# Where the W1 weights of a fused attention and MLP block are split: four pieces in the prologue, nineteen in the value stage, five in the Q and K stage

## The chip, the core and the metric

The kernel runs on one core of one Trainium2 chip. The metric is the time of one execution on the device, in microseconds (us). The core has TensorE (PE; PEld is its weight load), VectorE (DVE), ScalarE (ACT), GpSimd (POOL) and SyncE (SP), which mostly issues DMAs. Transfers are issued on the queues of SP and ACT and run on 16 DMA engines.

## The reference

For a sequence of 2048 tokens of width 1024, with 32 heads of 32 and an MLP of width 3584:

```python
xn = _layernorm(x, axis=-1)
s = _A_ref(xn, A_wqkv, A_wo)          # softmax attention, 32 heads, then @ wo
g = _silu(_B_ref(xn, B_w1, B_b1, B_w2))   # h = xn @ w1 + b1; mish(h) @ w2
return x + s * g
```

All inputs are float32.

## The kernel before

Every float32 matrix product is done as three products of a reduced float32 format (F32R): each operand is split into a high part (a copy that rounds) and a low part (the operand minus the high part, `low`), and high x high, high x low and low x high are added. Weights are split once, stored in DRAM in split form, and read back when needed. The first linear layer's weight W1 has 28 pieces (`FT`) of 1024 x 128: a piece is 512 KB raw and 1 MB split, in `w1s[f]`. W2 is split into 14 groups (`u`), of seven tiles each (`pw2`), because the second layer uses a scheme with seven products of half blocks.

The kernel has these stages.

- **Prologue** (to about 72 us). For each of 16 tiles of 128 tokens `t`: x is loaded on SP (`x_load`, a ring of five buffers), DVE takes mean and variance (`ln_a`: two bn_stats, one bn_aggr, one add), ACT the reciprocal root (`ln_r`), DVE corrects it by four instructions on one column (`ln_b`, lines 369 to 372), ACT normalizes (`ln_x`), PE transposes (`ln_t`), and ACT and DVE write the split xn into the chunk tile `xc[t // 4]` (`ln_c`: two copies, two subtracts). `xc[c]` holds 512 tokens, high part in `[:, 0]`, low part in `[:, 1]`. In between PE computes the first quarter of V (`v_group(0, ..)`). From t = 8 on, finished chunks are stored to DRAM (`xs`).
- **Value stage** (to 214 us). The other three quarters of V, `for i in range(1, 4)`, 16 groups each of 24 matmuls. After each group, `w1_early(step)` does a part of splitting W1 piece f = step // 2: on even steps it loads piece f and splits piece f - 1 on POOL (two casts and two subtracts, `split_w(.., job=True)`); on odd steps it stores the split piece. The split form goes into a buffer from `w_tile`, which hands out two places in turn: `z0` in the pool `w1p` and `w` in the pool `big`. The split Q and K weights (`qkw`) take their buffers from the same two. `W1_V = 21` pieces are done here.
- **Q and K stage** (to 640 us). 16 weight tiles f by 4 chunks c: `qk_group(f, c)` is 24 matmuls; ACT copies the result to `qst` (two buffers), DVE makes the low part, and ACT issues the store. After group (f, 0) ACT and DVE split the next weight tile (`qk_split(f + 1)`) and ACT issues the load of the one after it. Beside this POOL splits W2 group u = f (`w2_parts`, steps 0 to 3 after groups 0 to 3) for f up to 13, and half a W1 piece after each of the first 2 x (28 - 21) = 14 weight tiles (`presplit`: a load of 256 KB, a cast, a subtract, a store of 512 KB). For f of 12 and more PE also does four score matmuls of head 0 after each group.
- **The long stage** (from 640 us). Attention scores, exponentials, the MLP and the output product run together in an order that a planner in the program works out beforehand from fixed costs. The last part multiplies with Wo and forms the output.

The order of the work in the first three stages is the order in which the program is written. Each engine takes its instructions in that order. The DMAs of SP and ACT together, in program order, take eight completion semaphores in turn, and a DMA waits until the one before it on the same semaphore has landed; so a DMA of ACT can wait for one that SP issued eight places earlier, and the other way round. `later.at(n, fn)` moves an issue n groups on.

Of the kernel before, what the change touches and what calls it, by code (L numbers as in the profile page):

```python
# [9 lines left out]
F32 = mybir.dt.float32  # L10
F32R = mybir.dt.float32r
# [7 lines left out]
P = 128  # L19
KT = D // P  # L20
# [3 lines left out]
SCALE = DH ** -0.5  # L24
EPS = 1e-5

W1_V = 21
NS = H * NT
U = FT // 2

# [191 lines left out]
def body(ctx: ExitStack, tc: tile.TileContext, x, wqk, wv, wo, w1, b1, w2, out):  # L222
    nc = tc.nc
# [6 lines left out]
    def pool(stack, name, bufs, side="left", **kw):  # L230
        return stack.enter_context(tc.tile_pool(name=name, bufs=bufs, side=side, reuse_waits="tile", **kw))
# [8 lines left out]
    w1s = [dram.tile([P, 2, 2, KT // 2, P], F32R, name=f"w1s{i}") for i in range(FT)]  # L240
# [26 lines left out]
    w1p = pool(low_, "w1p", 1)  # L267
# [5 lines left out]
    def copy(out_, in_, scale=1.0):  # L273
        nc.scalar.activation(out_, in_, AF.Copy, scale=scale)  # L274

    def move(out_, in_, eng=None):

        (eng or nc.sync).dma_start(out_.bitcast(F32), in_.bitcast(F32))

    def low(eng, out_, in_, high):  # L280

        eng.tensor_tensor(out_, in_, high.bitcast(F32), ALU.subtract)  # L282
# [5 lines left out]
    def w_tile(name):  # L288
        w_made.append(name)
        where, tag = ((w1p, "z0"), (big, "w"))[len(w_made) % 2]  # L290
        return where.tile([P, 2, 2, KT // 2, P], F32R, tag=tag, name=name)
# [5 lines left out]
    big = pool(ph, "big", 1)  # L297
    ps1 = psum(ph, "ps1", 8)
    xc = [xc0] + [big.tile([P, 2, KT, 512], F32R, name=f"xc{c}") for c in range(1, NC)]
# [5 lines left out]
    def v_load(i):  # L305
        raws = []
        for half in range(2):
            raw = vp.tile([P, 4, 256], F32, tag="x", name=f"vraw{i}_{half}", bufs=5)
            nc.sync.dma_start(raw, wv[i][:, half * 4:half * 4 + 4])
            raws.append(raw)  # L310
        return raws
# [27 lines left out]
    def x_load(t):  # L339
        xt = vp.tile([P, D], F32, tag="x", name=f"x{t}", bufs=5)  # L340
        nc.sync.dma_start(xt, x[t * P:(t + 1) * P, :])
        return xt

    xts = {t: x_load(t) for t in range(2)}
    vraw = v_load(0)
    xts[2] = x_load(2)
# [19 lines left out]
    def ln_b(t):  # L366
        mv, var, rs = stat.pop(t)
        tmps[t] = tmp = vp.tile([P, 1], F32, tag="tmp", name=f"tmp{t}", bufs=3)
        nc.vector.scalar_tensor_tensor(tmp, rs, var, rs, op0=ALU.mult, op1=ALU.mult)
        nc.vector.tensor_scalar(tmp, tmp, -0.5, 1.5, op0=ALU.mult, op1=ALU.add)  # L370
        nc.vector.tensor_tensor(rs, rs, tmp, ALU.mult)
        nc.vector.scalar_tensor_tensor(tmp, mv[:, 0:1], -1.0, rs, op0=ALU.mult, op1=ALU.mult)
        tmps[t] = tmp, rs
# [44 lines left out]
    for t in range(2, NT + 2):  # L418
        if t < NT:
            ln_b(t)  # L420
        evac = v_group(0, vw, t - 2, 12 if t == 2 else 8, (lambda: ln_t(t - 1)) if t <= NT else None)
        if t <= NT:
            ln_c(t - 1)
        if t < NT:
            ln_x(t)
        for m in (4, 5, 6) if t == 2 else (t + 4,):
            if m < NT:
                xts[m] = x_load(m)
        if t == 2:
            ln_a(3)  # L430
        if t + 2 < NT:
            ln_a(t + 2)
        if t + 1 < NT:
            ln_r(t + 1)
        evac()
        if t == NT - 3:
            vraw = v_load(1)
        if t > 7:
            c, k = t // 4 - 1, t % 4 * 2
            move(xs[c][:, :, k:k + 2], xc[c][:, :, k:k + 2])  # L440
        if t == NT:
            nvw = v_split(1, vraw)
            vraw = v_load(2)
# [6 lines left out]
        raws[f] = big.tile([P, KT, P], F32, tag="raw", name=f"qkraw{f}")  # L450
        (nc.scalar if f > 1 else nc.sync).dma_start(raws[f], wqk[f])

    def split_w(w, raw, job=False):
        for half in range(2):
            r = slice(half * 4, half * 4 + 4)
            if job:
                nc.gpsimd.tensor_copy(w[:, half, 0], raw[:, r])
            else:
                copy(w[:, half, 0], raw[:, r])
            low(nc.gpsimd if job else nc.vector, w[:, half, 1], raw[:, r], w[:, half, 0])  # L460

    qkw = {}

    def qk_split(f):
# [4 lines left out]
    early_w1 = {}  # L469

    def w1_early(step):
        f, late = divmod(step, 2)
        if not late:
            if f < W1_V:
                raw = vp.tile([P, KT, P], F32, tag="x", name=f"w1e{f}", bufs=5)
                nc.sync.dma_start(raw, w1[f])
                early_w1[f] = [raw, None]
            if 0 < f <= W1_V:
                raw, _ = early_w1[f - 1]
                early_w1[f - 1][1] = w = w_tile(f"w1p{f - 1}")  # L480
                split_w(w, raw, True)
        elif 0 < f <= W1_V:
            move(w1s[f - 1], early_w1.pop(f - 1)[1])

    for i in range(1, 4):
        vw = nvw
# [107 lines left out]
    sp = pool(qb, "sp", 2, side="right")  # L594
    jobs = iter([(f, half) for f in range(W1_V, FT) for half in range(2)])

# [71 lines left out]
    for f in range(2 * KT):  # L668
        for c in range(NC):
            qk_group(f, c if f < 2 * KT - 1 else (c + 1) % NC)  # L670
            if f < U:
                w2_parts(f, c)
                if c == 3 and f + 2 < U:
                    later.at(1, lambda u=f + 2: w2_load(u))
            if c == 3 and f < 2 * (FT - W1_V):
                presplit()
# [690 lines left out]
    for c in range(NC):  # L1367
        for s in range(4):
            t = 4 * c + s
            if t + 4 < NT:  # L1370
                start(t + 4)
            for dh in range(2):
                k = 2 * s + dh
# [4 lines left out]
                if c:  # L1378
                    n = 2 * s + dh
# [53 lines left out]
```

## Time and profile before

| | |
|---|---|
| median of 3 runs | 3469.04 us (3467.42 to 3472.01) |
| profiled execution | 3470.76 us, span from first to last instruction 3469.0 us |
| PE busy | 3376.7 us, 97% of the span |
| POOL busy | 2792.7 us, 81% |
| DVE busy | 2614.4 us, 75% |
| ACT busy | 2017.0 us, 58% |
| DMA traffic | 639.92 MB, mean 184 GB/s |

Busy shares are means over stages with different limits, so the profile is read by stages here. A row of a group reads: line, engine, operation, what it writes and reads, shapes, count, then busy us and mean ns of one, then the idle time before it and what ended it. A row of the timeline begins with its start and its duration in us; the bracket at its end is the idle time of the engine before it and what released it. `SPq` and `ACTq` are the queues on which DMAs are issued.

### The profile page before, as it was taken

What the parts mean: (1) busy time and instruction counts of PE and PEld (TensorE: products, weight loads), DVE (VectorE), ACT (ScalarE), POOL (GpSimd) and SP (SyncE); (2) the same over time, 40 slices, a digit from 0 to 9 for tenths busy, and PEclk for the clock granted to TensorE, in tenths of its full rate; (3) what the DMA queues carried; (4) which work ended last, traced back from release to release, by engine and by line L of the source; (5) the groups of instructions that cost most, each with busy time, mean ns of one, the idle gap of its engine ahead of it and who ended that gap; (6) DMA issues with size and microseconds to landing.
All of it is one profiled execution on the core that took longest, in us unless ns stands there. A gap on an engine that the chain in (4) does not pass through costs nothing.

```text
span 3469.0 us, 48684 instructions
## 1 busy us (share of the span) xinstructions
PE 3376.7 (97%) x17491; PEld 2474.8 (71%) x17491; DVE 2614.4 (75%) x4382; ACT 2017.0 (58%) x3360; POOL 2792.7 (81%) x1033
## 2 busy tenths in 40 slices
PE   8999898999999999999999999999999999999999
PEld 8987676776776666666677666666766666667687
DVE  6012124799999998888989988888999889996653
ACT  6111111476766666767667667666766777677621
POOL 0749984489898888998989899989988999999910
PEclk9999998999999999999999999999999999999999
DMA  8869997444555556554545664445546545556582
GB/s 293 318 240 346 348 359 251 137 138 131 147 152 153 153 149 210 156 154 139 153 138 158 195 183 140 134 134 152 153 146 189 178 138 152 150 160 192 165 308 85
DMA packets 255189, 639.92 MB, mean 184 GB/s; under 512 B 89994, under 2 KB 99210, under 8 KB 244106
## 3 DMA queue, kind: packets, MB, share of 16 engines
q1 hardware_dynamic: 233076, 587.52, 54.6%
q10 hardware_dynamic: 21872, 49.29, 3.9%
q8 instruction: 139, 2.28, 0.3%
q14 instruction: 102, 0.84, 0.1%
HBM read 474.97 MB, written 160.69 MB: 183 GB/s over the span
## 4 chain that ended last, share of the span: by engine, by line
PE 78%; POOL 8%; DVE 6%; DMA 4%; ACT 2%; issue 1%; SPq 1%; ACTq 0%; POOLq 0%; DVEq 0%
PE h L982 16%; PE y L1123 13%; PE pv L871 12%; PE s L736 12%; PE t L823 12%; PE v L329 5%; PE op L1250 4%; POOL pw L282 3%; PE qk L657 3%; DVE mx L742 2%; POOL pw L625 1%; POOL tmp L636 1%; DMA kstack<-ks 1%; POOL z L852 1%; DVE yacc L1146 1%
## 5 line engine op out<-in xcount | busy, mean ns | idle before, releaser
L852 POOL TENSOR_TENSOR z<-z,p 128x2048 f32<-128x2048 f32 x448 | 2067.1, 4614 | 74.7 <-ACT p L271 50.2
L271 ACT ACTIVATE p<-t,zero 128x512 f32<-128x512 f32 x2048 | 1366.1, 689 | 457.2 <-PE t L823 436.9
L742 DVE TENSOR_REDUCE mx<-s 128x1 f32<-128x512 f32 x1984 | 1284.1, 683 | 67.7 <-PE s L736 65.3
L823 PE MATMUL t<-qstack,kstack 128*128 128x512 f32 x2048 | 791.7, 394 | 1.8 <-ACT p L271 0.9
L736 PE MATMUL s<-kstack,qstack 128*128 128x512 f32 x1984 | 756.1, 397 | 16.2 <-DMA kstack<-ks 7.3
L982 PE MATMUL h<-xr,w 128*128 128x512 f32 x2016 | 677.3, 390 | 1.5 <-DVE aw L282 0.6
L1146 DVE TENSOR_TENSOR yacc<-yacc,y 128x512 f32<-128x512 f32 x728 | 493.0, 680 | 40.4 <-PE y L1123 36.9
L736 PEld LDWEIGHTS s<-kstack,qstack 128*128 128x128 f32 x1984 | 367.0, 188 | 163.0 <-issue 31.5
L823 PEld LDWEIGHTS t<-qstack,kstack 128*128 128x128 f32 x2048 | 381.8, 188 | 126.4 <-issue 28.5
L871 PE MATMUL pv<-p,v 128*32 128x512 f32 x4096 | 467.2, 596 | 1.3 <-ACT p L271 0.6
L982 PEld LDWEIGHTS h<-xr,w 128*128 128x128 f32 x2016 | 377.9, 188 | 84.7 <-DVE aw L282 2.1
L657 PE MATMUL qk<-xc,qkw 128*128 128x512 f32 x1536 | 368.9, 401 | 29.6 <-ACT qkw L274 26.3
L657 PEld LDWEIGHTS qk<-xc,qkw 128*128 128x128 f32 x1536 | 296.6, 194 | 99.1 <-ACT qkw L274 29.3
L852 POOL TENSOR_TENSOR z<-p,p 128x2048 f32<-128x2048 f32 x32 | 147.8, 4620 | 217.5 <-PE zp L907 111.9
L871 PEld LDWEIGHTS pv<-p,v 128*32 128x32 f32 x4096 | 120.1, 110 | 277.7 <-issue 248.6
L282 DVE TENSOR_TENSOR qst<-qk,qst 128x512 fp32r<-128x512 f32 x64 | 44.3, 692 | 307.6 <-ACT qst L274 307.6
L274 ACT ACTIVATE qst<-qk 128x512 fp32r<-128x512 f32 x64 | 38.3, 598 | 370.5 <-PE qk L657 97.5
L1123 PE MATMUL y<-w,az 128*128 128x512 f32 x672 | 232.5, 395 | 4.2 <-POOL az L282 1.6
L1123 PE MATMUL y<-w,ay 128*128 128x512 f32 x672 | 229.0, 395 | 3.5 <-ACT ay L274 1.4
L1123 PE MATMUL y<-w,ax 128*128 128x512 f32 x672 | 224.8, 391 | 2.6 <-DVE yacc L1146 1.4
L982 PE MATMUL h<-xc,w 128*128 128x512 f32 x672 | 225.9, 391 | 0.0
L329 PE MATMUL v<-vw,xc 128*128 128x256 f32 x1536 | 190.8, 285 | 2.7 <-POOL vw L282 1.5
(117 smaller groups left out, 3659.9 us busy)
## 6 DMA issues: line engine op xcount, KB each, us to landing
w<-w2s SPq DMA_DIRECT2D x392, 512.0 KB
w<-w1s SPq DMA_DIRECT2D x224, 512.0 KB
w2s<-pw SPq DMA_DIRECT2D x98, 512.0 KB
qstack<-qs SPq DMA_DIRECT2D x96, 256.0 KB
kstack<-ks SPq DMA_DIRECT2D x96, 256.0 KB
w1s<-w1p SPq DMA_DIRECT2D x21, 1024.0 KB
x<-in_A_x_dram SPq DMA_DIRECT2D x32, 512.0 KB
qs<-qst ACTq DMA_DIRECT2D x32, 512.0 KB
```

What stands on the lines that cost most here:

```text
L271: nc.scalar.activation(out_, in_, fn, bias=zero if bias is None else bias, scale=scale)
L282: eng.tensor_tensor(out_, in_, high.bitcast(F32), ALU.subtract)
L329: nc.tensor.matmul(ps[:, :256], xc[t // 4][:, a, k, (t % 4) * P:(t % 4 + 1) * P], w[:, b, k], start=n == 0, stop=n == 3 * KT - 1)
L657: nc.tensor.matmul(ps, w[:, k // 4, a, k % 4], xc[c][:, b, k], start=n == 0, stop=n == 3 * KT - 1)
L736: nc.tensor.matmul(sp_, qst[h % 3][:, qt * P:(qt + 1) * P], kst[h % 3][:, kc * 512:(kc + 1) * 512], start=True, stop=True)
L742: nc.vector.reduce_max(tiles["mx"][:, qt, kc:kc + 1], tiles[qt, kc], axis=AX.X)
L823: nc.tensor.matmul(tp, kst[h % 3][:, kt * P:(kt + 1) * P], qst[h % 3][:, c * 512:(c + 1) * 512], start=True, stop=True)
L852: nc.gpsimd.tensor_tensor(zs[h], pts[T - 1] if kt == 1 else zs[h], pts[T], ALU.add)
L871: nc.tensor.matmul(t["b"][c * DH:(c + 1) * DH, :], vt[h][:, k, :], pts[T - kt + k][:, c * 512:(c + 1) * 512], start=k == kt - size + 1, st ...
L982: nc.tensor.matmul(t["h"], w1t[m_][:, a, k % 4], xts_[c][:, b, k], start=i == 0, stop=i == 3 * KT - 1)
L1123: nc.tensor.matmul(t["y"], acts[B, kind][:, p, half * 256 + s * P:half * 256 + (s + 1) * P], w2t[m_][:, q], start=i == 0, stop=i == 2)
L1146: nc.vector.tensor_tensor(ya, ya, t["y"], ALU.subtract)
```

## The change

`W1_0, W1_V = 4, 23`. Pieces 0 to 3 are loaded in the prologue (t = 2 to 5), split on POOL one token tile later (t = 3 to 6) and stored three tiles after the load (t = 5 to 8) by the new `w1_first`. Their raw form lies in the two `w_tile` places, their split form in the low halves of the chunk tiles `xc[2]` and `xc[3]`, which the prologue writes from t = 9 on. The value stage does pieces 4 to 22. Every third of them (f % 3 == 2) uses two half tiles from the ring `w1` of three, which the later stages use anyway, in place of a `w_tile` buffer. The Q and K stage keeps five pieces, ten halves. PE, DVE and ACT execute the same instructions in the same order as before.

```diff
--- before.py
+++ after.py
@@ -24,7 +24,7 @@
 SCALE = DH ** -0.5
 EPS = 1e-5
 
-W1_V = 21
+W1_0, W1_V = 4, 23
 NS = H * NT
 U = FT // 2
 
@@ -341,6 +341,30 @@
         nc.sync.dma_start(xt, x[t * P:(t + 1) * P, :])
         return xt
 
+    first_w1 = [p.tile([P, 2, KT, P], F32, tag=tag, name=f"w1f{tag}") for p, tag in ((w1p, "z0"), (big, "w"))]
+
+    def split_w(w, raw, job=False):
+        for half in range(2):
+            r = slice(half * 4, half * 4 + 4)
+            p = w[half] if isinstance(w, list) else w[:, half]
+            if job:
+                nc.gpsimd.tensor_copy(p[:, 0], raw[:, r])
+            else:
+                copy(p[:, 0], raw[:, r])
+            low(nc.gpsimd if job else nc.vector, p[:, 1], raw[:, r], p[:, 0])
+
+    def w1_first(n, step):
+        t, g = xc[2 + n // 2], n % 2
+        raw = first_w1[n // 2][:, g]
+        w = t[:, 1, 4 * g:4 * g + 4].rearrange("p k n -> p (k n)") \
+            .rearrange("p (h a k f) -> p h a k f", h=2, a=2, f=P)
+        if step == 0:
+            nc.sync.dma_start(raw, w1[n])
+        elif step == 1:
+            split_w(w, raw, True)
+        else:
+            move(w1s[n], w)
+
     xts = {t: x_load(t) for t in range(2)}
     vraw = v_load(0)
     xts[2] = x_load(2)
@@ -433,6 +457,9 @@
         if t + 1 < NT:
             ln_r(t + 1)
         evac()
+        for step, n in enumerate((t - 2, t - 3, t - 5)):
+            if 0 <= n < W1_0:
+                w1_first(n, step)
         if t == NT - 3:
             vraw = v_load(1)
         if t > 7:
@@ -450,15 +477,6 @@
         raws[f] = big.tile([P, KT, P], F32, tag="raw", name=f"qkraw{f}")
         (nc.scalar if f > 1 else nc.sync).dma_start(raws[f], wqk[f])
 
-    def split_w(w, raw, job=False):
-        for half in range(2):
-            r = slice(half * 4, half * 4 + 4)
-            if job:
-                nc.gpsimd.tensor_copy(w[:, half, 0], raw[:, r])
-            else:
-                copy(w[:, half, 0], raw[:, r])
-            low(nc.gpsimd if job else nc.vector, w[:, half, 1], raw[:, r], w[:, half, 0])
-
     qkw = {}
 
     def qk_split(f):
@@ -469,18 +487,26 @@
     early_w1 = {}
 
     def w1_early(step):
-        f, late = divmod(step, 2)
+        f, late = W1_0 + step // 2, step % 2
         if not late:
             if f < W1_V:
                 raw = vp.tile([P, KT, P], F32, tag="x", name=f"w1e{f}", bufs=5)
                 nc.sync.dma_start(raw, w1[f])
-                early_w1[f] = [raw, None]
-            if 0 < f <= W1_V:
-                raw, _ = early_w1[f - 1]
-                early_w1[f - 1][1] = w = w_tile(f"w1p{f - 1}")
-                split_w(w, raw, True)
-        elif 0 < f <= W1_V:
-            move(w1s[f - 1], early_w1.pop(f - 1)[1])
+                early_w1[f] = raw
+            if W1_0 < f <= W1_V:
+                f -= 1
+                raw = early_w1.pop(f)
+                if f % 3 == 2:
+                    w = [w1p.tile([P, 2, KT // 2, P], F32R, tag="w1", name=f"w1h{f}_{i}", bufs=3) for i in range(2)]
+                    split_w(w, raw, True)
+                    early_w1[f] = [(w1s[f][:, i], w[i]) for i in range(2)]
+                else:
+                    w = w_tile(f"w1p{f}")
+                    split_w(w, raw, True)
+                    early_w1[f] = [(w1s[f], w)]
+        elif W1_0 < f <= W1_V:
+            for args in early_w1.pop(f - 1):
+                move(*args)
 
     for i in range(1, 4):
         vw = nvw
```

SP's queue in the prologue around the token tiles t = 5 to 8, before (`x` are loads of token tiles, `vs0` stores of V, the first number in a name is the tile or piece):

```order
L335 DMA vs0_78<-vst0_2_389 128x256
L341 DMA x9_490<-in_A_x_dram 128x1024
L335 DMA vs0_78<-vst0_3_449 128x256
L341 DMA x10_550<-in_A_x_dram 128x1024
L335 DMA vs0_78<-vst0_4_509 128x256
L341 DMA x11_610<-in_A_x_dram 128x1024
```

and now (`w1fw` is a raw piece of W1, `w1s0` the split piece 0 in DRAM):

```order
L335 DMA vs0_78<-vst0_2_397 128x256
L362 DMA w1fw_180<-in_B_w1_dram 128x1024
L341 DMA x9_503<-in_A_x_dram 128x1024
L335 DMA vs0_78<-vst0_3_462 128x256
L362 DMA w1fw_180<-in_B_w1_dram 128x1024
L278 DMA w1s0_82<-xc2_174 128x2048
L341 DMA x10_569<-in_A_x_dram 128x1024
L335 DMA vs0_78<-vst0_4_528 128x256
L278 DMA w1s1_83<-xc2_174 128x2048
L341 DMA x11_634<-in_A_x_dram 128x1024
```

A load of a raw piece stands ahead of the x loads of tiles 7 to 10 and a store of a split piece ahead of those of tiles 10 to 13.

SP's queue at the end of the value stage, before (`vst3` are the last quarter's V tiles, `raw2` raw W2, `zeros` follows POOL's memset of `qstack0`):

```order
L278 DMA w1s19_101<-w1p19_2501 128x2048
L335 DMA vs3_81<-vst3_10_2535 128x256
L335 DMA vs3_81<-vst3_11_2568 128x256
L278 DMA w1s20_102<-w1p20_2563 128x2048
L335 DMA vs3_81<-vst3_12_2597 128x256
L335 DMA vs3_81<-vst3_13_2625 128x256
L335 DMA vs3_81<-vst3_14_2653 128x256
L335 DMA vs3_81<-vst3_15_2681 128x256
L278 DMA zeros_139<-qstack0_2713 32x2048
L621 DMA raw2_0_2726<-in_B_w2_dram 128x2048
```

and now:

```order
L335 DMA vs3_81<-vst3_7_2471 128x256
L278 DMA w1s22_104<-w1p22_2466 128x2048
L478 DMA qkraw1_2505<-in_A_wqk_dram 128x1024
L335 DMA vs3_81<-vst3_8_2507 128x256
L335 DMA vs3_81<-vst3_9_2535 128x256
L335 DMA vs3_81<-vst3_10_2563 128x256
L335 DMA vs3_81<-vst3_11_2591 128x256
L335 DMA vs3_81<-vst3_12_2619 128x256
L335 DMA vs3_81<-vst3_13_2647 128x256
L335 DMA vs3_81<-vst3_14_2675 128x256
L335 DMA vs3_81<-vst3_15_2703 128x256
L278 DMA zeros_139<-qstack0_2735 32x2048
```

The last split piece is stored after V group 7 of the last quarter, before the split of qkw0 is issued; before it was stored after group 11, and its buffer was the one that qkw0 had taken.

POOL in the Q and K stage at W2 group 12, before:

```order
L282 TENSOR_TENSOR pw2_12_0_4731<-raw2_12_4536,pw2_12_0_4731 128x512
L625 CAST pw2_12_2_4734<-raw2_12_4536 128x512
L282 TENSOR_TENSOR pw2_12_2_4734<-raw2_12_4536,pw2_12_2_4734 128x512
L611 CAST pw26_1_4755<-praw26_1_4696 128x512
L282 TENSOR_TENSOR pw26_1_4755<-praw26_1_4696,pw26_1_4755 128x512
L636 TENSOR_TENSOR tmp2_12_4730<-raw2_12_4536 128x512
```

and now:

```order
L282 TENSOR_TENSOR pw2_12_0_4745<-raw2_12_4556,pw2_12_0_4745 128x512
L651 CAST pw2_12_2_4748<-raw2_12_4556 128x512
L282 TENSOR_TENSOR pw2_12_2_4748<-raw2_12_4556,pw2_12_2_4748 128x512
L662 TENSOR_TENSOR tmp2_12_4744<-raw2_12_4556 128x512
L651 CAST pw2_12_5_4803<-tmp2_12_4744 128x512
```

The cast and the subtract of half a W1 piece are gone at W2 groups 10 to 13; groups 0 to 9 keep theirs.

## The prediction

> **What bounds the kernel now.** I read three views in this order: the page's share of each engine, a table by stretches cut at the stage borders (prologue to 72 us, value stage to 214, Q and K stage to 640, then the long stage), and inside the slow stretch the waits and the timeline. The table's columns are the stretch, its length, the busy time of PE, PEld, DVE, ACT and POOL (with instruction counts), the granted PE clock, the DMA engines' share and the GB/s they moved.
>
> ```profile
> span 3469.0 us, 48684 instructions
> 20.00:44.00 24.00, 23.44 (x201) 23.24 (x199) 22.60 (x69) 19.82 (x41) 0.00 (x0) 1.00 0.57 179
> 44.00:92.00 48.00, 46.48 (x391) 46.08 (x390) 21.51 (x60) 25.76 (x51) 4.72 (x2) 1.00 1.02 390
> 92.00:214.00 122.00, 122.00 (x1019) 122.00 (x1018) 1.65 (x2) 20.08 (x48) 84.18 (x84) 1.00 0.88 318
> 214.00:244.00 30.00, 30.00 (x137) 24.95 (x136) 5.78 (x8) 2.02 (x4) 5.56 (x5) 1.00 0.14 54
> 244.00:562.00 318.00, 275.33 (x1126) 219.77 (x1126) 70.16 (x85) 42.36 (x74) 286.00 (x278) 0.92 0.96 349
> 562.00:640.00 78.00, 78.00 (x346) 64.60 (x345) 41.01 (x72) 9.95 (x21) 1.90 (x2) 1.00 0.46 151
> 640.00:3469.00 2829.00, 2791.19 (x14230) 1964.93 (x14228) 2438.99 (x4050) 1886.35 (x3108) 2407.21 (x655) 1.00 0.53 159
> ```
>
> From 640 us on PE is busy 2791 of 2829 us with an order that the change leaves alone, so whatever is won or lost before 640 us shifts the end by as much. Only one stretch has PE waiting: from 244 to 562 us it is busy 275 of 318 us at a granted clock of 0.92, while the DMA engines are at 0.96 and POOL is busy 286 us. Just before it, from 214 to 244 us, the DMA engines stand nearly still (0.14).
>
> What the stage would take without waits follows from PE's own rows: eight groups without scores in 43.71 us, and a group with four score matmuls every 6.35 us (563.51 to 569.86).
>
> ```profile
> 214.56 43.71 PE L657 MATMUL qk<-xc,qkw 128*128 128x512 f32 x192
> 563.51 0.91 PE s L554 x4
> 569.86 0.91 PE s L554 x4
> ```
>
> That is 48 x 5.46 + 16 x 6.35 = 364 us for 64 groups, against 640 - 214.5 = 425.5 us: some 62 us are stall or slow clock. The waits of the stretch from 240 to 562 us say what they hang on (engine and line, what it waited for, total, times, longest):
>
> ```profile
> ACT qst L274 <- DMA w2s<-pw: 72.2, 13, 11.3
> ACT qst L274 <- DMA ks<-qst: 67.1, 13, 13.6
> ACT qst L274 <- DMA qs<-qst: 60.6, 9, 10.7
> PEld qk L657 <- ACT qkw L274: 29.3, 7, 10.2
> PE qk L657 <- ACT qkw L274: 26.3, 7, 9.7
> ACT qst L274 <- DMA w1s<-w1p: 23.1, 1, 23.1
> ```
>
> PE waits for ACT's split of the next weight tile, and ACT stands behind DMAs: its own stores and, through the eight shared completion semaphores, POOL's stores of W2. The stage is paced by the DMA engines, and its DMA work started late. The timeline says why:
>
> ```profile
> 208.25 1.30 POOL L282 TENSOR_TENSOR w1p<-w1e,w1p 128x512 fp32r<-128x512 f32 x1
> 236.58 0.61 POOL L457 CAST w1p<-w1e 128x512 fp32r<-128x512 f32 x1 [27.04 <-PE qk L657]
> 240.55 1.80 POOL L514 MEMSET qstack<- 32x2048 f32 x1
> 240.93 3.17 SPq L335 DMA_DIRECT2D vs<-vst  x4
> 244.69 1.69 SPq L621 DMA_DIRECT2D raw<-in_B_w_dram  x2
> 252.47 0.61 POOL L625 CAST pw<-raw 128x512 fp32r<-128x512 f32 x1 [10.11 <-DMA raw<-in_B_w_dram]
> 561.18 0.32 SPq L278 DMA_DIRECT2D w2s<-pw  x1
> ```
>
> Piece 20 needs the buffer that qkw0 holds, so POOL sits 27 us until PE is through with the first weight tile (236.6). On SP its store stands ahead of the last V stores and of the first W2 loads, which go out at 244.7 instead of right after the value stage. The last W2 store is issued at 561.2.
>
> **The change part by part.** *End of the value stage.* The order has piece 22 split and stored while eight V groups are still to come, before qkw0 asks for a buffer. POOL's memset then waits only for the last V matmul: 214.5, plus 1.8 us of memset, plus the 2.3 us that lay between its end and the W2 loads (242.35 to 244.69), gives W2 loads at 218.6, some 26 us earlier.
>
> *The Q and K stage.* Two pieces, four half jobs, leave it. The sizes of one transfer each:
>
> ```profile
> w1s<-w1p SPq DMA_DIRECT2D x21, 1024.0 KB
> w1e<-in_B_w_dram SPq DMA_DIRECT2D x21, 512.0 KB
> w1s<-pw SPq DMA_DIRECT2D x14, 512.0 KB
> praw<-in_B_w_dram SPq DMA_DIRECT2D x14, 256.0 KB
> ```
>
> Four halves are 4 x 768 KB = 3.1 MB, and piece 20's store, 1.05 MB, falls before the stage. The stage moved 30 x 54 + 318 x 349 GB/s = 112.6 MB up to 562 us. 108.4 MB remain, at 349 GB/s 310.6 us; begun at 218.6 they end at 529.2 instead of 562. POOL's side is cheaper by four times a cast and a subtract (rows below), 4 x 1.99 = 8 us, and begins 26 us earlier too, so it does not hold the DMAs back. If PE stands at the same place of the order when the W2 stores end (78 us from the border, as now), the border moves by **-32.8 us**, to 607. This is above PE's own floor of 214.5 + 364 = 578.
>
> The bounds of this term: PE cannot gain more than 62 us (no stall left). It gains least if it is further behind when W2 is done. Now it had a lead, since it did two whole weight tiles (the 192 matmuls) against idle DMA engines; if it ends one weight tile (21.9 us) further back, 10.9 us are left. I take the middle case: the eight semaphores keep ACT and SP within eight DMAs of each other in either kernel, about half a weight tile of the order.
>
> *The prologue.* POOL gets 16 instructions where it did nothing (0.00 busy from 20 to 44 us), 4 x 2 x (0.61 + 1.29) = 15.2 us, one piece of 3.8 us for each token tile of some 3.6 us: hidden as POOL's own time, but not for DVE, which is busy 22.6 of those 24 us and hands its result straight to PE:
>
> ```profile
> 25.65 0.16 DVE L372 SCALAR_TENSOR_TENSOR tmp<-mv,rs 128x1 f32<-128x1 f32 x1
> 25.72 1.28 DVE L282 TENSOR_TENSOR xc<-pt,xc 128x512 fp32r<-128x512 f32 x2
> ```
>
> Three DVE instructions a tile (L369, L371, L372) read two tensors in SBUF. What such a one costs beside POOL, the trace has in the Q and K stage and at the end (first row: mean; second: shortest, median, longest; then POOL's two kinds):
>
> ```profile
> L282 DVE TENSOR_TENSOR qkw<-qkraw,qkw 128x512 fp32r<-128x512 f32 x32 | 35.8, 1157 | 129.4 <-ACT qkw L274 129.4
> L282 DVE TENSOR_TENSOR qkw<-qkraw,qkw x32: 679/1092/1776, 200.6 to 597.1; 128x512 fp32r<-128x512 f32 x32
> L611 POOL CAST pw<-praw 128x512 fp32r<-128x512 f32 x14 | 9.5, 676 | 5.9 <-DMA praw<-in_B_w_dram 5.9
> L282 POOL TENSOR_TENSOR pw<-praw,pw 128x512 fp32r<-128x512 f32 x14 | 18.3, 1309 | 1.1
> ```
>
> Against the shortest, the mean wait is 1157 - 679 = 0.48 us, the longest 1.10. Twelve such instructions (three in each of four tiles) cost 12 x 0.48 = **5.7 us**, with 0 (none waits: they are only 0.16 us long) and 12 x 1.10 = 13.2 us as bounds; a gain is excluded, as nothing is removed there. I take the mean, since POOL's instructions there are the same two kinds.
>
> The Trainium skill speaks against the change here: SBUF — State Buffer, section "Who interferes with whom", says that a DVE instruction with two SBUF inputs contends with a GpSimd instruction that reads SBUF, and that the loser is blocked until the other is through. If each of the twelve waited for a whole POOL subtract it would be 12 x 1.31 = 15.7 us and the sum 3452; the 1776 ns row agrees with blocking, and the mean of 1157 says that a wait is a part of an instruction.
>
> The prologue's DMAs: 4 x (0.52 + 1.05) = 6.3 MB are added, and 20 to 44 us has 24 x 0.43 x 314 GB/s (179 at a share of 0.57) = 3.2 MB free. The rest, 3.1 MB, queues for 7.9 us at 390 GB/s, into the stretch that is full already. An x load has more time than that, from issue to first use:
>
> ```profile
> 43.53 0.55 SPq L341 DMA_DIRECT2D x<-in_A_x_dram  x1
> 52.41 1.28 DVE L356 BATCH_NORM_STATS2 st<-x 128x6 f32<-128x512 f32 x2
> ```
>
> That is 8.9 us. I count nothing for it; were it late, the cost is the queue at most, 7.9 us. The V weights of the next pass and the first pieces of the value stage come as much later, and that stage has 0.12 of its 122 us, 14.6 us of DMA time, to catch up in, plus two pieces fewer. The longer ring only changes which buffer a piece uses: one store of 1 MB becomes two of 0.5 MB on SP, 0.3 us more of issue for each of six pieces, beside PE's 122 us of uninterrupted matmuls.
>
> **Sum.** 3469.0 - 32.8 + 5.7 = 3441.9 us of span. The profiled execution took 3470.76, 1.8 us more than its span, and the median of the runs is 3469.04, 1.7 below that execution: the median forecast is 3442 us.
>
> **The rivals.** *A, the forecast*, 3425 to 3455: chance 0.57.
>
> *B, no stall is left.* If the earlier start lets PE run at its own rate, the border is at 578 and the time 3469 - 62 + 5.7 = 3413. For it: POOL starts level with PE, and PE's 21.9 us a weight tile is near POOL's pace. Against it: a weight tile with its share of W2 and W1 moves 8.1 MB, 23 us at 349 GB/s, more than PE needs. Chance 0.15.
>
> *C, the start is only moved.* PE loses its two tiles done against idle DMA engines and ends one weight tile further back: 3469 - 10.9 + 5.7 = 3464. For it: ACT fell behind POOL's stores over the stage now, by the 200 us of DMA waits above. Against: eight semaphores bound how far. Chance 0.18.
>
> *D, slower: POOL blocks DVE in the prologue for more than the two-input instructions.* If all eight SBUF-to-SBUF instructions of a tile wait for a POOL subtract, four tiles cost 32 x 1.31 = 42 us and the time is 3469 + 42 - 32.8 = 3478. It decides from a mean wait of 1.03 us on. Against it stands a bn_stats pair that ran beside POOL's first V subtract and took 1.28 us, as others do:
>
> ```profile
> 12.94 2.40 POOL L282 TENSOR_TENSOR vw<-vraw,vw 128x1024 fp32r<-128x1024 f32 x1 [11.63 <-ACT vw L274]
> 13.32 1.28 DVE L356 BATCH_NORM_STATS2 st<-x 128x6 f32<-128x512 f32 x2
> ```
>
> Chance 0.06.
>
> *E, the change does not do what it says*: piece 22 is still late and POOL waits again, only the 3.1 MB (9 us) are saved: 3466. The order speaks against it. Chance 0.04.
>
> **How the numbers follow.** A measurement of this kernel tells about 0.2%, 7 us, from no change. Faster is A, B and half of C, 0.81; within 7 us the other half of C and E, 0.13; slower D, 0.06. The range from 3412 to 3465 holds A, most of B and over half of C; A's own is 3425 to 3455.
>
> **What would show it.** POOL's first W2 cast near 225 us plus the prologue's delay instead of 252.5, and no 27 us wait before a W1 cast; DMA share above 0.9 right from about 220 us; the last W2 store near 535; the first score matmul of the long stage near 613. In the prologue L369, L371 and L372 lengthened in four tiles, PE waiting for DVE's xc there, the bn_stats not lengthened and not waiting for x. The forecast is wrong if the Q and K stage keeps its 425 us, or if the value stage ends more than 13 us later than 214.5.

## The result, and the profile after

The changed kernel takes 3450.8 us in the median (3448.7 to 3453.8 in 4 runs) where the kernel before, run beside it, takes 3470.5 (3467.4 to 3472.0): a ratio of 0.9945, 95% interval 0.9928 to 0.9962, so 13 to 25 us less. The profiled execution has a span of 3452.0 us against 3469.0.

The table by stretches of the changed kernel, with the prediction's columns and borders (a line of kernel.py that stood behind line 341 has a number up to 27 higher than before):

```profile
span 3452.0 us, 48687 instructions
20.00:44.00 24.00, 22.80 (x189) 22.11 (x188) 22.97 (x62) 18.96 (x39) 14.93 (x16) 1.00 0.92 316
44.00:92.00 48.00, 44.02 (x356) 43.41 (x355) 22.92 (x67) 26.13 (x50) 4.72 (x2) 0.96 1.02 396
92.00:214.00 122.00, 122.00 (x1019) 122.00 (x1018) 1.57 (x2) 20.61 (x48) 82.31 (x81) 1.00 0.89 316
214.00:244.00 30.00, 30.00 (x158) 25.85 (x157) 8.27 (x11) 4.59 (x9) 16.37 (x16) 1.00 0.78 279
244.00:562.00 318.00, 293.19 (x1235) 237.39 (x1234) 79.16 (x102) 43.52 (x77) 265.54 (x257) 0.95 0.94 335
```

The 30 us in which the DMA engines stood still (0.14) now run at 0.78. From 244 to 562 us PE is busy 293 us instead of 275. In the prologue PE loses about 3 us (66.8 us busy from 20 to 92 us instead of 69.9). The timeline shows the new start of W2:

```profile
209.10 1.80 POOL L540 MEMSET qstack<- 32x2048 f32 x1
219.90 2.46 PE L683 MATMUL qk<-xc,qkw 128*128 128x512 f32 x10
221.45 1.22 SPq L647 DMA_DIRECT2D raw<-in_B_w_dram  x2
226.96 1.00 POOL L651 CAST pw<-raw 128x512 fp32r<-128x512 f32 x1 [16.06 <-DVE qst L282]
```

The first W2 cast starts at 226.96 instead of 252.47, and no W1 cast waits 27 us. The value stage, however, ends at 219.90 instead of 214.56. The stage's end is the last group of score matmuls in it; here it is with the range of the W2 stores' issues (a row of the view by tile: shortest, median and longest, then first and last start), of the kernel before:

```profile
L278 SPq DMA_DIRECT2D w2s<-pw x98: 319/320/1244, 254.5 to 561.2; - x98
639.65 1.07 PE L554 MATMUL s<-kstack,qstack 128*128 128x512 f32 x4
```

and of the changed one:

```profile
L278 SPq DMA_DIRECT2D w2s<-pw x98: 319/320/969, 229.7 to 530.0; - x98
620.20 1.07 PE L580 MATMUL s<-kstack,qstack 128*128 128x512 f32 x4
```

| | before | changed | difference |
|---|---|---|---|
| end of the value stage | 214.56 | 219.90 | +5.3 |
| last W2 store issued | 561.2 | 530.0 | -31.2 |
| last scores of the Q and K stage | 639.65 | 620.20 | -19.5 |
| from there to the end of the span | 2829.4 | 2831.8 | +2.4 |
| span | 3469.0 | 3452.0 | -17.0 |

W2 is done 31 us earlier, but PE's border moves by 19.5 only: from the last W2 store to the border it was 78.5 us and is now 90.2. What ACT waits for from 240 to 562 us has hardly changed (before, in the order of the first three rows: 72.2, 60.6 and 67.1 us):

```profile
ACT qst L274 <- DMA w2s<-pw: 77.9, 13, 9.7
ACT qst L274 <- DMA qs<-qst: 64.3, 11, 10.9
ACT qst L274 <- DMA ks<-qst: 61.0, 11, 11.6
PEld qk L683 <- ACT qkw L274: 10.7, 4, 4.5
```

So three questions were left: which part of the change brought the gain, what the prologue's 5.3 us are, and what holds the Q and K stage at 400 us (219.9 to 620.2) where PE needs 364.

### The profile page after: what moved, and what is told of

It is laid out like the page before. It is cut to its first block, busy times and chain, and to the rows that moved or that the text cites. A ratio compares the mean times of both kernels' runs of the same rounds, so it can differ in the third digit from the quotient of the medians.

```text
span 3452.0 us, 48687 instructions
## 1 busy us (share of the span) xinstructions
PE 3372.2 (98%) x17491; PEld 2474.5 (72%) x17491; DVE 2616.3 (76%) x4382; ACT 2017.9 (58%) x3360; POOL 2794.2 (81%) x1033
## 4 chain that ended last, share of the span: by engine, by line
PE 78%; POOL 8%; DVE 7%; DMA 4%; ACT 2%; issue 1%; SPq 0%; ACTq 0%; POOLq 0%; DVEq 0%
PE h L1008 16%; PE y L1149 13%; PE pv L897 12%; PE s L762 12%; PE t L849 12%; PE v L329 4%; PE op L1276 4%; POOL pw L282 3%; PE qk L683 2%; DVE mx L768 2%; POOL pw L651 1%; POOL tmp L662 1%; POOL z L878 1%; DMA praw<-in_B_w_dram 1%; DVE yacc L1172 1%
## 5 line engine op out<-in xcount | busy, mean ns | idle before, releaser
L683 PEld LDWEIGHTS qk<-xc,qkw 128*128 128x128 f32 x1536 | 293.7, 192 | 78.5 <-ACT qkw L274 10.7
```

The source lines that it names most:

```text
L683: nc.tensor.matmul(ps, w[:, k // 4, a, k % 4], xc[c][:, b, k], start=n == 0, stop=n == 3 * KT - 1)
```

## The experiments

Ratios are against the kernel before, run on the same chip beside each set, with a 95% interval. Groups of the Q and K stage are numbered 0 to 63 (4f + c), and "the border" is the start of the last scores of that stage.

### Which part brings the gain

**One number alone.** In the kernel before:

```diff
-W1_V = 21
+W1_V = 20
```

> The kernel before with W1_V = 20 in place of 21: one piece less in the value stage, one more (two halves) in the Q and K stage, nothing in the prologue, the old buffers. Piece 19, now the last, takes the buffer that qkw0 does not hold. Theory 1 (the late last piece held back all of POOL's and the DMAs' work of the Q and K stage): POOL's 27 us wait is gone, the first W2 cast comes near 222 us in place of 252.5, and although the stage moves 1.6 MB more for the extra piece, the time falls by 10 to 20 us, to 3449 to 3459. Theory 2 (the gain of the change comes from the two pieces that left the Q and K stage): one piece more there costs 1.6 MB, 4.5 us at 349 GB/s, so the time rises to about 3474.

Measured: 3447.1 us, 0.9944 (0.9932 to 0.9957). The value stage ends at 214.5, the border is at 616.0. The last piece is no longer late, there are eight pieces in the Q and K stage instead of seven, and the whole gain is there. What the change does beyond that brings nothing.

**The change without its prologue pieces**, with the longer ring:

```diff
-W1_0, W1_V = 4, 23
+W1_0, W1_V = 0, 20
```

> The changed kernel with W1_0, W1_V = 0, 20: no piece in the prologue, twenty in the value stage with the longer ring, eight in the Q and K stage. The prologue is then the one of before: V ends near 214.5 us in place of 219.8, 5.3 us earlier. If the early start is what pays (theory 1), the Q and K stage takes as long as in the changed kernel plus three pieces more, 4.7 MB or 13.5 us at 349 GB/s, and the time is 3451 - 5.3 + 13.5 = 3459, the same as with the old buffers and W1_V = 20. If the longer ring itself pays, it is 5 us or more below that run. If the pieces in the prologue are what pays (theory 2), it is near 3470.

Measured: 3448.8 us, 0.9942 (0.9928 to 0.9955); value stage to 214.6, border 616.5. Against the run above this leaves only the ring, and the two agree: the ring neither costs nor pays.

**Two pieces in the prologue:**

```diff
-W1_0, W1_V = 4, 23
+W1_0, W1_V = 2, 21
```

> The changed kernel with W1_0, W1_V = 2, 21: two pieces in the prologue in place of four, nineteen in the value stage, seven in the Q and K stage. If the prologue's loss comes from the DMA queue in front of the x loads (3.1 MB too much by the rows of before), half the pieces fit into what is free and the loss falls from 5.4 us to 1 to 2 us; if it comes from DVE blocked by POOL it falls to half, 2.7 us. Two pieces more in the Q and K stage cost 3.1 MB, 9 us at 349 GB/s, if that stage is paced by its DMAs alone, so 3451 - 4 + 9 = 3456; if the stage is paced by how ACT's and SP's DMAs wait for each other, less than 9 us, and the time is 3447 to 3452.

Measured: 3447.8 us, 0.9942 (0.9930 to 0.9955); value stage to 215.2, border 615.7. The prologue's loss is 0.7 us here, which fits the DMA queue (1 to 2 us expected) better than DVE blocked by POOL (2.7). So five, seven or eight pieces in the Q and K stage give stages of 400.3, 400.5 and 401.5 us. The prediction had priced a piece there at 4.5 us (1.57 MB at 349 GB/s); it costs about 0.4.

### What the prologue costs

**Its DMAs without POOL's work.** The pieces are loaded and stored as they are, so pieces 0 to 3 are not split.

```diff
         elif step == 1:
-            split_w(w, raw, True)
+            pass
         else:
-            move(w1s[n], w)
+            both = first_w1[n // 2].rearrange("p g k n -> p (g k n)")
+            move(w1s[n], both.rearrange("p (h a k f) -> p h a k f", h=2, a=2, f=P))
```

> The changed kernel with the four pieces of the prologue loaded and stored as now, but not split: POOL's sixteen instructions are left out and the stores take the raw pieces (so the first four W1 pieces are not what they should be). Theory of the forecast (DVE blocked by POOL, 5.7 us): the value stage ends near 214.5 in place of 219.8 us. Rival (the x loads come late behind the added DMAs): it still ends at 217 or later, with DVE waiting for x as in the changed kernel, and L393 to L396 back at 160 to 210 ns.

**POOL's work without the DMAs**, on a constant tile; pieces 0 to 3 are again left out (one more changed line, not printed, makes the MLP read piece 4 in their place).

```diff
         if step == 0:
-            nc.sync.dma_start(raw, w1[n])
+            if g == 0:
+                nc.gpsimd.memset(first_w1[n // 2], 0.5)
         elif step == 1:
             split_w(w, raw, True)
-        else:
-            move(w1s[n], w)
```

> The changed kernel with POOL's 16 casts and subtracts in the prologue, but on a constant tile (two memsets on POOL) and without the eight loads and stores, so pieces 0 to 3 are not split and the MLP reads piece 4 in their place. Theory of the prediction, POOL makes DVE's two-input instructions wait and that is the prologue's loss: V matmuls end 5 us later than before, near 220. Rival, the loss is late x loads: V matmuls end at 214.4 to 216.5, though L393, L395 and L396 keep their longer means (about 242, 271 and 159 ns), and DVE waits for x no longer than before (2.9 us).

With the DMAs alone the value stage ends at 220.7 (3453.2 us, one run), with POOL alone at 215.9 (3446.2 us, one run). DVE's groups from 20 to 72 us (busy, mean ns, idle before) of the kernel before:

```profile
L356 DVE BATCH_NORM_STATS2 st<-x 128x6 f32<-128x512 f32 x24 | 15.3, 680 | 0.0
L369 DVE SCALAR_TENSOR_TENSOR tmp<-rs,var 128x1 f32<-128x1 f32 x13 | 2.7, 211 | 0.8 <-ACT rs L271 0.8
L371 DVE TENSOR_TENSOR rs<-rs,tmp 128x1 f32<-128x1 f32 x13 | 2.1, 159 | 0.4
```

of the changed one:

```profile
L380 DVE BATCH_NORM_STATS2 st<-x 128x6 f32<-128x512 f32 x24 | 15.3, 681 | 4.9 <-DMA x<-in_A_x_dram 4.9
L395 DVE TENSOR_TENSOR rs<-rs,tmp 128x1 f32<-128x1 f32 x13 | 3.9, 297 | 0.4
L393 DVE SCALAR_TENSOR_TENSOR tmp<-rs,var 128x1 f32<-128x1 f32 x13 | 3.2, 248 | 0.6 <-ACT rs L271 0.6
```

of the DMAs alone:

```profile
L381 DVE BATCH_NORM_STATS2 st<-x 128x6 f32<-128x512 f32 x24 | 15.4, 683 | 6.7 <-DMA x<-in_A_x_dram 6.7
L396 DVE TENSOR_TENSOR rs<-rs,tmp 128x1 f32<-128x1 f32 x13 | 2.1, 159 | 0.4
```

and of POOL alone:

```profile
L379 DVE BATCH_NORM_STATS2 st<-x 128x6 f32<-128x512 f32 x24 | 15.3, 681 | 0.0
L394 DVE TENSOR_TENSOR rs<-rs,tmp 128x1 f32<-128x1 f32 x13 | 3.2, 244 | 0.5
```

POOL lengthens DVE's two-input instructions and costs 1.3 us of the value stage's end; the DMAs make DVE wait for x and cost 6.1; together they cost 5.3. The two do not add up, but the value stage ends at 219.4 to 220.9 in the five profiles that have all of this prologue, so 6.1 and 5.3 are alike: the DMAs by themselves account for the whole loss. The late load stands in the changed kernel's timeline:

```profile
47.08 1.52 SPq L341 DMA_DIRECT2D x<-in_A_x_dram  x1
57.27 1.29 DVE L380 BATCH_NORM_STATS2 st<-x 128x6 f32<-128x512 f32 x2 [3.44 <-DMA x<-in_A_x_dram]
```

It is issued at 47.08 (43.53 in the kernel before) behind a 1 MB store of a W1 piece (44.51) and an xs store, and is used 10.2 us later, where the prediction counted on 8.9 us from issue to use.

### What holds the Q and K stage

**The store of Q and K issued at once**, in the changed kernel:

```diff
-        later.at(1, lambda: move(dst, st, nc.scalar))
+        move(dst, st, nc.scalar)
```

> The changed kernel, with the store of a Q or K group issued right behind its split instead of one group later. Theory 1, ACT's stores pace the Q and K stage: with two qst buffers and a store that is issued after the next group's copy, the copy after that waits for a landing (8 to 10 us where a group takes PE 5.46), so the stage takes 400 us and not PE's 364. Issued at once, two groups share one landing: the stage should fall by 20 to 36 us, the border from 620 to 584 to 600, the time from 3451 to 3415 to 3431, and ACT's waits for qs<-qst and ks<-qst (69 and 61 us) to less than half. Theory 2, the DMA engines or POOL pace it: the stage keeps 395 to 405 us and the time stays within 7 us of 3451. Theory 3: ACT, which now waits for DVE at each store, becomes late for the split of the next weight tile; the stage gets longer than 405 us.

Measured: 3451.9 us, 0.9953 (0.9939 to 0.9968); the stage takes 402 us. The run tells less than the expectation says: `later.at(1, ..)` issues at the end of the same group, not one group later, so three stores in four stand where they stood, right behind their split, and only the store of a weight tile's first group moves ahead of the split of the next tile. Theory 1 is hardly tested by it. The same edit with `W1_V = 20` in the kernel before:

> The kernel before with W1_V = 20 and the store of a Q or K group issued right behind its split. If theory 1 of the run on the changed kernel holds, and the prologue's pieces are not needed, this is the fastest of all: 20 to 36 us under the 3447 of the kernel with W1_V = 20 alone, 3411 to 3427. If the stage is paced by bytes or by POOL, whose eight pieces are more here, it stays at 3440 to 3450.

Measured: 3450.9 us, 0.9951 (0.9934 to 0.9968). No gain there either, and as little is tested.

**No W1 pieces in the stage**, in the changed kernel; pieces 23 to 27 are left out (one more changed line, not printed, makes the MLP read piece 22 in their place).

```diff
-            if c == 3 and f < 2 * (FT - W1_V):
-                presplit()
```

> The changed kernel without the ten half pieces of W1 in the Q and K stage (pieces 23 to 27 are not split and the MLP reads piece 22 in their place). Theory of the prediction, the stage is paced by its DMA bytes: 10 x 768 KB = 7.9 MB less at 349 GB/s are 22.5 us, the border falls from 620 to about 598, the time from 3451 to 3428. Rival, the stage is paced by ACT's wait for its own stores and the pieces cost next to nothing (8 pieces took 401 us, 5 took 400): the stage keeps 390 us or more and the time falls by at most 10 us.

Measured: 3447.5 us, 0.9941 (0.9926 to 0.9955), 3.4 us under the changed kernel and not 22.5. Its expectations were about rates, of bytes or of landings, and the profile shows why a rate is the wrong question:

```profile
L278 SPq DMA_DIRECT2D w2s<-pw x98: 319/320/1514, 230.7 to 501.9; - x98
504.89 0.39 ACTq L278 DMA_DIRECT2D ks<-qst  x1
614.71 1.07 PE L580 MATMUL s<-kstack,qstack 128*128 128x512 f32 x4
```

W2 is done 28 us earlier than in the changed kernel (501.9), but PE's border comes only 5.5 us earlier. The ACT store in the second row is that of group 44, and it goes out just when W2 is through. SP and POOL were by then 11 groups ahead of ACT, which eight semaphores in the order of the code, as the prediction had them, would not allow.

The answer is in the built program. It records all engines' instructions in one list, and the eight semaphores are handed out along this list, which is not the order of the code: W2's last tiles (code: behind groups 52 to 55) are recorded among Q and K stores of weight tiles 10 to 12. Why the build records them so is not shown here. From the changed kernel's list, each row an issue, its semaphore, the DMA, and the DMA that had the semaphore before and must land first:

```
SP   5  w2s13<-pw2_13_4   before it: w2s12<-pw2_12_3
SP   6  w2s13<-pw2_13_6   before it: w2s13<-pw2_13_0
SP   7  w2s13<-pw2_13_3   before it: ks5<-qst11_0
...
ACT  3  ks5<-qst11_3      before it: w2s13<-pw2_13_1
...
ACT  6  qs6<-qst12_0      before it: w2s13<-pw2_13_6
```

The store of group 48 (`qst12_0`) must wait for W2's last tile but one. (In the list of the run without pieces, the store of group 44 has W2's last store before it on its semaphore.) The timeline of the changed kernel shows it: its data are copied by 524.6, POOL finishes that tile at 525.97 and subtracts for the last one until 530.02, and ACT's queue stands still until the store goes out:

```profile
524.03 0.60 ACT L274 ACTIVATE qst<-qk 128x512 fp32r<-128x512 f32 x1 [6.84 <-DMA w2s<-pw]
524.70 1.27 POOL L282 TENSOR_TENSOR pw<-raw,pw 128x512 fp32r<-128x512 f32 x1
528.74 1.28 POOL L282 TENSOR_TENSOR pw<-tmp,pw 128x512 fp32r<-128x512 f32 x1
528.97 0.37 ACTq L278 DMA_DIRECT2D qs<-qst  x1
534.94 0.35 ACTq L478 DMA_DIRECT2D qkraw<-in_A_wqk_dram  x1
535.40 0.60 ACT L274 ACTIVATE qst<-qk 128x512 fp32r<-128x512 f32 x1 [9.73 <-DMA qstack<-zeros]
```

The next DMA of ACT, the weight load at 534.94, stands in the same way until `qstack<-zeros` has landed, which had its semaphore before and stands behind W2 on SP. Behind a waiting store or load stand ACT's copies, which free PE's banks. By this reading a kernel ends the stage at the end of W2 plus the groups recorded behind W2's last store. Two edits of one line each were made to move that place.

**Raw W2 loaded by ACT from group 2 on**, so that W2 cannot be recorded far ahead of ACT:

```diff
-        nc.sync.dma_start(raw2[u].rearrange("p (f d) n -> p f (d n)", f=2), w2[u])
+        (nc.scalar if u > 1 else nc.sync).dma_start(raw2[u].rearrange("p (f d) n -> p f (d n)", f=2), w2[u])
```

> The changed kernel, with the loads of raw W2 from group 2 on issued by ACT instead of SP, so that in the recorded order POOL's W2 groups cannot run far ahead of ACT's Q and K stores. New theory: the stage is tied by the completion semaphores in the order in which the build recorded the DMAs, not in program order. In the changed kernel the store of group 48 (the first of weight tile 12) takes its semaphore after one of the last W2 stores; it was issued at 528.97, 0.2 us after POOL's last W2 work, and 16 groups were left. Here that place is group 52 (weight tile 13), 4 groups later: with W2 done near 518 to 530 the rest is 12 x 6.35 = 76 us and some 5 of lag, the border falls from 620 to 594 to 606, the time from 3451 to 3425 to 3437. Rival, the DMA engines' bytes or POOL pace the stage whatever the semaphores: the same bytes and the same POOL work, so the stage keeps 395 us or more and the time stays within 7 us of 3451. Second rival: ACT, now blocked by the loads, is late for its splits, and the stage gets longer.

Measured: 3433.9 us, 0.9898 (0.9876 to 0.9919). POOL now waits for raw W2 (31 us in all, 20 of them before its first cast) and W2 ends 5 us later, but 14 stores are left behind its last one instead of 18:

```profile
L278 SPq DMA_DIRECT2D w2s<-pw x98: 319/320/641, 229.2 to 535.3; - x98
534.87 0.37 ACTq L278 DMA_DIRECT2D ks<-qst  x1
603.27 1.07 PE L580 MATMUL s<-kstack,qstack 128*128 128x512 f32 x4
```

The store of group 52, which in this kernel's list has W2's last store but one before it on its semaphore, goes out at the end of W2, as expected, and the border is at 603.3.

**Q and K stored by SP**, in the order of the code, between the W2 stores:

```diff
-        later.at(1, lambda: move(dst, st, nc.scalar))
+        later.at(1, lambda: move(dst, st))
```

> The changed kernel, with the stores of Q and K issued by SP instead of ACT, in program order between the W2 stores. In the recorded order the last W2 store then stands beside group 55 (weight tile 13), 7 groups later than in the changed kernel. Theory of the recorded semaphores: if W2 is still done near 530, 8 groups are left, 51 us and some lag, so the border is at 580 to 592 and the time 3411 to 3423; the price is that a W2 store waits for a Q or K store and the other way round, which can move W2's end: if that is 20 us later, 3431 to 3443. Rival, bytes or POOL pace the stage: it keeps 395 us or more, within 7 us of 3451.

Measured: 3416.1 us, 0.9847 (0.9829 to 0.9864), the fastest kernel of all; it beats the changed one by 35 us. W2 ends 8 us later, but only 8 stores are left behind its last one:

```profile
L278 SPq DMA_DIRECT2D w2s<-pw x98: 319/320/1202, 230.2 to 538.3; - x98
587.19 1.07 PE L580 MATMUL s<-kstack,qstack 128*128 128x512 f32 x4
244.00:500.00 256.00, 253.39 (x1112) 209.17 (x1112) 63.07 (x76) 40.02 (x70) 235.53 (x228) 1.00 0.98 365
500.00:530.00 30.00, 30.00 (x132) 24.77 (x131) 17.49 (x27) 3.52 (x7) 28.77 (x28) 0.98 0.82 320
```

From 244 to 500 us the DMA engines are at 0.98, as full as before, and PE is busy 253 of 256 us at full clock. The same bytes and the same POOL work now fit beside PE, so neither paced the stage; nor did the landing of Q and K's stores with two buffers (theory 1), which both kernels have. The stage takes 366.7 us, 3 more than the prediction's count of 364.

**The same line in the kernel before:**

> The kernel before (21 pieces in the value stage, none in the prologue, the last piece late), with the stores of Q and K issued by SP in program order. Theory: W2 still starts some 26 us late, and now SP holds Q and K's first stores behind W2's first ones too, so the border is near the start of W2 (252.5) plus about 300 us of W2 plus the 8 groups and lag (60 us), 605 to 615 instead of 640, and the time 3434 to 3446: the change is then still worth 20 to 30 us against the changed kernel with the same edit (3416). Rival, with the semaphores out of the way the late start no longer matters: the border comes to 585 and the time to 3412 to 3420, as PE never waits.

Measured: 3436.1 us, 0.9897 (0.9883 to 0.9912). W1's last piece still waits, and W2 still starts late:

```profile
236.50 0.61 POOL L457 CAST w1p<-w1e 128x512 fp32r<-128x512 f32 x1 [28.91 <-PE qk L657]
L278 SPq DMA_DIRECT2D w2s<-pw x98: 319/320/1263, 252.5 to 556.3; - x98
605.20 1.07 PE L554 MATMUL s<-kstack,qstack 128*128 128x512 f32 x4
```

The change is worth 20 us with this line (3436.1 to 3416.1; 17 us by the two ratios), about as much as without it.

**And with `W1_V = 20` in the kernel before:**

> The kernel before with W1_V = 20 and the stores of Q and K issued by SP in program order: the start of W2 mended by one number, no prologue pieces, no longer ring, eight pieces in the Q and K stage. Theory: the value stage ends at 214.5 instead of 220, and POOL's pace of some 21.5 us a weight tile with a piece's half in it is still under PE's 21.9, so the border is at 580 to 588 and the time 3407 to 3416, up to 8 us under the changed kernel with the same edit. Rival, three more pieces now cost their bytes or POOL time, 3 x 4.5 us, since no wait hides them: the border is at 592 to 600 and the time 3420 to 3430.

Measured: 3418.6 us, 0.9847 (0.9830 to 0.9863). The border, 586.2, is where the theory had it; the time is between the theory's range and the rival's. The value stage ends 6.0 us earlier than in the changed kernel with this line, the Q and K stage takes 371.8 us instead of 366.7: now that no wait hides them, three pieces more cost 5 us (one profile of each), about as much as the prologue's pieces cost there. The two ways come out alike.

The place and what follows from it, by the number of Q and K stores recorded behind the last W2 store (the runs left out have 16 or 18, and 81 to 94 us between):

| kernel | stores behind | last W2 store | border | between |
|---|---|---|---|---|
| changed, no pieces in the stage | 22 | 501.9 | 614.7 | 112.8 |
| changed | 18 | 530.0 | 620.2 | 90.2 |
| before, W1_V = 20 | 16 | 534.9 | 616.0 | 81.1 |
| before | 15 | 561.2 | 639.7 | 78.5 |
| changed, raw W2 by ACT | 14 | 535.3 | 603.3 | 68.0 |
| changed, Q and K by SP | 8 | 538.3 | 587.2 | 48.9 |
| before, Q and K by SP | 8 | 556.3 | 605.2 | 48.9 |
| before, W1_V = 20, Q and K by SP | 8 | 537.3 | 586.2 | 48.9 |

The time between follows the place: divided by the number of stores it is 4.9 to 6.1 us. The W1 pieces do lengthen W2 itself: from its first to its last store it takes 271.2, 300.3 and 311.4 us with 0, 10 and 16 half pieces in the stage. But with fewer of them the last W2 store also stands further from the end of the list (22, 18 and 16 stores behind it), so PE gains little. Each of the two edits moves DMAs to another queue as well as another place; that the wait is the semaphore's alone, and not also the queue's, was not tried apart.

## Why the prediction was right or wrong

Forecast 3442, measured 3450.8: right in direction, inside the range, 9 us too low. By the terms of the sum, the Q and K stage became 24.8 us shorter (425.1 to 400.3) and not 32.8, the prologue cost 5.3 and not 5.7, and 2.4 us more passed behind the border.

**What bounds the kernel: right in place, wrong in kind.** Whatever is lost before the border shifts the end, up to 2.4 us. The late start of W2 was the cause of the gain: one number removes it and gives 20 us. But "the stage is paced by the DMA engines" is wrong: with the same bytes the stage takes 366.7 us. A DMA share of 0.96 and long DMA waits showed that transfers were many and slow to land, not that they were the bound.

**End of the value stage: right.** W2's loads were forecast at 218.6 plus 5.7 and went out at 221.5; the first cast was forecast near 231 and started at 227.0. One step was wrong: POOL's memset did not wait for the last V matmul, it ran at 209.10; the W2 loads waited on SP behind the last V stores.

**The Q and K stage: the step that failed is "if PE stands at the same place of the order when the W2 stores end (78 us from the border, as now)".** W2's end itself was forecast at 535 and came at 530: from its loads to its last store it took 308.6 us where the bytes gave 310.6 (whether bytes or POOL's work set this, no run tells apart). The place moved by three stores (15 behind W2's last to 18), and with it the distance from 78.5 to 90.2 us. The middle case rested on semaphores given in the order of the code, as the description of the kernel and the prediction both state it, and the recorded list refutes that: the bound of "eight DMAs" holds along the list, not along the code. The border was forecast 27.1 us earlier (32.8 less the prologue's 5.7) and moved by 19.5.

The 3.1 MB that leave the stage, 9 us in the sum, were worth next to nothing to PE: with seven and five pieces it took 400.5 and 400.3 us.

**The prologue: right in size by luck, wrong in cause.** Forecast 5.7, measured 5.3: one term was too large, and one that was put at nothing made up for it. The 5.7 us were put on DVE's two-input instructions, which by themselves cost 1.3 us of the end; late x loads, for which the prediction counts nothing and 7.9 us at most, cost 6.1. So its sign "the bn_stats not lengthened and not waiting for x" held in the first half and failed in the second. Over 13 tiles L395 lost 13 x 0.138 = 1.8 us and L393 0.5 us, where 12 x 0.48 had been counted. The Trainium skill, SBUF — State Buffer, section "Who interferes with whom", has the loser blocked until the other is through. The trace agrees: in the five tiles beside POOL's work seven of fifteen such instructions were longer than usual, and each ended within 0.03 us of the end of a POOL instruction, the longest here:

```profile
40.52 1.29 POOL L282 TENSOR_TENSOR xc<-w1fw,xc 128x512 fp32r<-128x512 f32 x1
40.67 1.15 DVE L395 TENSOR_TENSOR rs<-rs,tmp 128x1 f32<-128x1 f32 x1
```

But each waited only for the rest of one POOL instruction, 0.15 to 1.0 us, so the 15.7 us of twelve whole ones did not come.

**What was hidden: right.** POOL's 15 us cost at most the 1.3 us above, and the later loads and the split stores of the value stage cost PE nothing from 92 to 214 us (122.00 of 122). The ring was free.

**Rivals.** B (no stall left) did not come with this change; its time, 3413, is what one more line gives (3416). C described what happened, PE further back when W2 ends, in about half its size (11.7 of 21.9 us), though not for its reason, ACT falling behind POOL's stores. D did not come: no bn_stats got longer (681 ns against 680). E did not come.

## What to carry to other kernels

When two engines issue DMAs that share completion semaphores, look up the order in which the build hands these out before pricing an edit: a queue that waits for another engine's transfer looks, in the waits and in the DMA share, like a lack of bandwidth. Test a bound by taking its load away: three pieces more, or all pieces out, changed the stage by 1 to 7 us of 400, where the bytes said 14 to 23. And before a many-part change is built, try its smallest part: here one number had the whole gain.

## What the hardware showed that was not expected

PE's stalls cost more than their length. The changed kernel, 515 to 540 us:

```profile
515.00:520.00 5.00, 0.80 (x1) 0.29 (x1) 0.69 (x1) 0.60 (x1) 4.71 (x6) 0.78 1.01 387
520.00:525.00 5.00, 0.00 (x0) 0.00 (x0) 0.34 (x1) 0.97 (x2) 4.78 (x6) 0.50 0.37 146
530.00:532.00 2.00, 2.00 (x6) 1.57 (x5) 0.58 (x1) 0.00 (x0) 0.01 (x1) 0.50 1.04 400
532.00:534.00 2.00, 2.00 (x6) 1.52 (x6) 0.00 (x0) 0.00 (x0) 0.00 (x0) 0.50 1.13 301
534.00:536.00 2.00, 2.00 (x9) 1.60 (x8) 0.00 (x0) 0.60 (x1) 0.00 (x0) 0.78 0.99 213
536.00:540.00 4.00, 4.00 (x19) 3.33 (x18) 3.97 (x7) 0.60 (x1) 0.00 (x0) 1.00 1.01 205
```

While PE has almost nothing to do the granted clock falls to 0.50, and it stays there until about 535 us, some 5 us into uninterrupted work. The Trainium skill, TensorE: Matmul & The Clock Gate, section "Part 1: The HAM clock gate", gives half the clock when idle and the full one after at least one busy window of some 3.4 us. The trace agrees on the half, and the 5 us are more than one such window. Over the stage of the changed kernel, and then of the one with Q and K stored by SP:

```profile
220.00:620.00 400.00, 375.19 (x1598) 305.22 (x1597) 116.84 (x164) 54.22 (x98) 281.90 (x272) 0.96 0.84 299
```

```profile
220.50:588.50 368.00, 365.32 (x1605) 301.70 (x1603) 118.72 (x165) 54.98 (x100) 282.10 (x272) 1.00 0.89 325
```

Of the 32 us between them 22 are idle (24.8 against 2.7), and 10 are the same matmuls at a slower clock (375.2 us busy against 365.3).
